# A fused attention and two-layer-block kernel: block 0's GpSimd low parts go to VectorE, all absolute values and q's readouts to ScalarE, and batch 1's attention is placed earlier

## The chip, the cores and the metric

The kernel runs on one core of a Trainium2 chip. The metric is device time in microseconds (us) of that core. The program has five engines that matter here: TensorE (PE; its weight loads are PEld), VectorE (DVE), ScalarE (ACT), GpSimd (POOL) and SyncE (SP), which issues the DMAs.

## The reference

All inputs arrive as 64-bit floats, which the kernel reads as pairs of 32-bit words. What is computed, cut to its core:

```python
p_packed = sm_attn(p, k, v)              # 32 packed queries for each head; softmax over 576 tokens
out = sm_attn(q, p_packed, p_packed)     # 576 queries over 32 packed keys; 8 batches, 8 heads of 64
x = out.transpose(0, 2, 1, 3)            # 4608 tokens x 512
h = x @ w_in                             # 512 -> 2048
g = np.where(h > 0, h, exp(min(h, 0)) - 1)
x2 = g @ w_out                           # 2048 -> 512
y = ((x2 @ w_a) * (x2 @ w_b)) @ w_out2   # 512 -> 1536 -> 512
```

## The kernel before, in words

The first part works by batch: eight blocks of 32 steps. A step takes one half h of a batch's tokens (288) and one slice f of 128 of the 2048 hidden columns. It makes `h` = w_in' a (`l1`, line 458, six matmuls: high x high, high x low, low x high over two row groups), the activation (`act1`: ge on ScalarE, lines 466 and 467, gf on VectorE, line 470, its high part gr on ScalarE, line 472, its low part, line 474) and, two steps later, the second layer (`l2`, line 480: twelve matmuls into four accumulators x2a). Every fp32 product is three products of high and low parts. In block 0 the slices come in two halves, so that the first steps need only a part of the weights: steps 0 to 15 take f 0 to 7 of both token halves, steps 16 to 31 take f 8 to 15. A tile `h0_0_8` is that of batch 0, half 0, f 8, and so of step 16.

The products of w_in with the packed values (`wp`, line 245, four for each batch, wp0_0 to wp0_3 for batch 0) take the place of w_in in the first layer: each is read out by ScalarE (line 82) and VectorE (line 83) into a ring `wr` of five pairs. So l1 of four steps waits for one wp. The attention of batch b + 1 runs within block b: score products (s1), exponentials e, their transposes (aT), packed values (pp, line 306, and its readout pps, line 320), their transposes (ppT), the second scores (s2), a softmax over 32 keys (lines 343 to 370), and the four wp. The tiles pT, s1, aT, pp, ppT, s2 and wp share one pair of PSUM banks (`pair_of_banks`, one buffer).

Block 0 also converts the weights of the first part from 64-bit words: `convert`, 16 tiles of w_in (`win`) and 16 of w_out (`wm_o`), 128 x 512 each. Step u0 takes the absolute value of the high word, two of three on ScalarE (line 134), the third on VectorE (line 136), and scales the low word on ScalarE; u1 clamps (line 140) and shifts (line 141); u2 puts the sign in (line 144) and adds the low word on GpSimd (line 147); u3, for w_out alone, splits into a high part (ScalarE, line 151) and a low part (line 152). The low parts of w_out, and those of gr in every second step of block 0, are computed by GpSimd. The transposed q is read out of PSUM in `qkT_tokens` (line 214), alternately by ScalarE and VectorE.

The order of the work: each piece has a time in half steps (`put`), two for each step, with block b's step s at 64b + 2s; `run_until` emits what is due as the steps go by, and a piece whose chain is stuck waits. `issue_until` emits what a step needs if it has not come yet. Batch 1's attention stands at 24 + 0.9t for its own times t from 0 to 64, and its last items (t > 64) at t + 2.3. In block 0 the order on each engine is then the framework scheduler's; from block 1 on TensorE, VectorE and ScalarE keep the order of the code.

After the eight blocks comes the second part (lines 808 to 860), which no edit touches.

Of the kernel before, what the change touches and what calls it, by code (L numbers as in the profile page):

```python
# [16 lines left out]
U32 = mybir.dt.uint32  # L17
# [3 lines left out]
P = 128  # L21
# [4 lines left out]
def program(tc, q, k, v, p, w_in, w_out, w_a, w_b, w_out2, out):  # L26
# [8 lines left out]
    nc = tc.nc  # L35
# [25 lines left out]
    with ctx:  # L61
# [4 lines left out]
        stage = ctx.enter_context(tc.tile_pool(name="stage", bufs=NSTAGE))  # L66
# [4 lines left out]
        at = at_stack.enter_context(tc.tile_pool(name="at", bufs=1, reuse_waits="tile"))  # L71
# [15 lines left out]
        wout_r = [w1.tile([P, 2, DM], F32R, name=f"wout{f}") for f in range(NF)]  # L87
# [4 lines left out]
        win = at.tile([P, NJ, FF], F32, name="win")  # L92
# [27 lines left out]
                )  # L120
            return t

        def convert(t, key, mags, dst=None, parts=None, pool_lo=True, on_act=True, store=None):

            w = t.bitcast(U32).rearrange("p (n t) -> p n t", t=2)
            low, high = w[:, :, 0], w[:, :, 1]
            pool, n = mags
            m = pool.tile([P, 512], U32, tag="wmag", name=f"wm_{key}", bufs=n) if dst is None else dst  # L130

            def u0():
                if on_act:
                    nc.scalar.activation(m.bitcast(F32), high.bitcast(F32), AF.Abs)
                else:
                    nc.vector.tensor_scalar(m, high, 0x7FFFFFFF, None, ALU.bitwise_and)
                nc.scalar.activation(low.bitcast(I32), low, AF.Copy, scale=2.0 ** -29)

            def u1():
                nc.vector.tensor_scalar(m.bitcast(F32), m.bitcast(F32), F64_MIN, F64_MAX, ALU.max, ALU.min)  # L140
                nc.vector.tensor_scalar(m, m, 3, 0x3FFFFFF8, ALU.logical_shift_left, ALU.bitwise_and)

            def u2():
                nc.vector.scalar_tensor_tensor(  # L144
                    m, high, 0xC0000000, m, op0=ALU.bitwise_and, op1=ALU.bitwise_or
                )
                nc.gpsimd.tensor_tensor(m.bitcast(I32), m.bitcast(I32), low.bitcast(I32), op=ALU.add)

            def u3():
                f = m.bitcast(F32)  # L150
                nc.scalar.copy(parts[:, 0, :], f)
                (nc.gpsimd if pool_lo else nc.vector).tensor_tensor(
                    parts[:, 1, :], f, parts[:, 0, :].bitcast(F32), op=ALU.subtract
                )

            def u4():
                nc.sync.dma_start(store, m.bitcast(F32))

            return [u0, u1, u2] + ([] if parts is None else [u3]) + ([] if store is None else [u4])
# [35 lines left out]
        def qkT_tokens(b, which, jj):  # L195

            if jj == 0:
                st[b, which + "T"] = at.tile([P, NJ, S], F32, tag="qkT", name=f"{which}T{b}")
            dst = st[b, which + "T"]
            t, tail = st[b, which, jj]  # L200
            for i in range(2):
                o = bank("h", 2, f"{which}Tp{b}_{jj}{i}")
                for c in range(4):
                    for r in range(2):
                        nc.tensor.matmul(
                            o[r * D:(r + 1) * D, c * P:(c + 1) * P],
                            t[:, 2 * i + r, c, :],
                            ident,
                            start=True,
                            stop=True,  # L210
                            tile_position=(0, r * D),
                        )
                copy = nc.vector.tensor_copy if i else nc.scalar.copy
                copy(
                    dst[:, 2 * jj + i, :4 * P].rearrange("p (n c) -> p c n", c=4),
                    o.rearrange("p (c n) -> p c n", c=4),
                )
            o = bank("h", 2, f"{which}Tt{b}_{jj}")
            n = S - 4 * P
            for i in range(2):  # L220
                nc.tensor.transpose(o[:, i * n:(i + 1) * n], tail[:, i * P:(i + 1) * P], ident[:n, :n])
            nc.vector.tensor_copy(
                dst[:, 2 * jj:2 * jj + 2, 4 * P:], o[:, :2 * n].rearrange("p (i n) -> p i n", i=2)
            )
# [236 lines left out]
                    n += 1  # L461
            return t

        def act1(t, key, run, pool_lo=False):
            e = m1.tile([P, HS], F32, tag="ge", name=f"ge{key}")
            nc.scalar.activation(e, t[:, :HS], AF.Relu, scale=-1.0)  # L466
            nc.scalar.activation(e, e, AF.Exp, scale=-1.0)  # L467
            run(0)
            g = m1.tile([P, HS], F32, tag="gf", name=f"gf{key}")
            nc.vector.scalar_tensor_tensor(g, e, -1.0, t[:, :HS], op0=ALU.add, op1=ALU.max)  # L470
            gr = m1.tile([P, 2, HS], F32R, tag="gr", name=f"gr{key}", bufs=4)
            nc.scalar.copy(gr[:, 0, :], g)  # L472
            run(1)
            (nc.gpsimd if pool_lo else nc.vector).tensor_tensor(gr[:, 1, :], g, gr[:, 0, :].bitcast(F32), op=ALU.subtract)  # L474
            return gr

        def l2(acc, f, gr, first, last):
# [65 lines left out]
                clock[0] += 1  # L543
                run_until(clock[0])

        def conveyor(convs, mags, late, on_act):


            convs = sorted(convs, key=lambda x: x[0])
            words = {}  # L550

            def load(i):
                if i < len(convs):
                    words[i] = load_words(convs[i][1], convs[i][2])

            def step(i, n):
                _, _, key, dst, parts, pool_lo = convs[i]
                if n == 0:
                    words[i] = convert(words[i], key, mags[i % len(mags)], dst, parts, pool_lo, bool(on_act) and i % on_act != 0)
                if n < len(words[i]):  # L560
                    words[i][n]()
                    if n + 1 == len(words[i]):
                        done.add(key)
                if n == 2:
                    load(i + NSTAGE)

# [39 lines left out]
        for n, (kind, x, j) in enumerate(order):  # L606
            if n < 4:
                t = -44 + 4 * n
            elif n < 16:
                t = -34 + 1.5 * (n - 4)  # L610
            else:
                t = 12 + 2.5 * (n - 16)
            if kind == "i":
                convs.append((t, w_in[j * P:(j + 1) * P, x * 512:(x + 1) * 512], f"i{x}_{j}",
                              win[:, j, x * 512:(x + 1) * 512].bitcast(U32), None, True))
            else:
                convs.append((t, w_out[x * P:(x + 1) * P, :], f"o{x}", None, wout_r[x], True))
        conveyor(convs, [(stage, 2), (at, 1), (stage, 2)], 4, 3)
        for b in range(1, B):
            for t, fn, takes, frees in attention(b):  # L620
                late = t > 64
                if b == 1:
                    t = 24 + 0.9 * max(t, 0) if not late else t + 2.3
                put(2 * NF * 2 * (b - 1) + t, fn, chain=(b, late), takes=takes, frees=frees)


        def m1_block(b):
            half = NF // 2 if b == 0 else NF
            order = [(h, f) for f0 in range(0, NF, half) for h in range(2) for f in range(f0, f0 + half)]
            for s, (h, f) in enumerate(order):  # L630
                first, last = f % half == 0, f % half == half - 1
                if first:
                    acc = []
                t0 = 4 * NF * b + 2 * s
                t = l1(b, h, f)
                gr = act1(t, f"{b}_{h}_{f}", lambda n: run_until(t0 + n), b == 0 and s % 2 == 0)
                pend.append((b, h, f, gr, acc, first, last, f // half + 1 if half < NF else 0))
                if len(pend) > 2:
                    run_pend()
# [293 lines left out]
```

## Time and profile before

| | |
|---|---|
| median of three runs | 1662.57 us (1661.4, 1662.57, 1662.66) |
| the profiled execution | 1660.11 us, span 1658.1 us |
| PE busy | 1576.9 us (95%), PEld 1442.4 us (87%) |
| DVE busy | 1034.2 us (62%) |
| ACT busy | 710.3 us (43%) |
| POOL busy | 206.3 us (12%) |

The first five of the profile's 40 slices of 41.5 us have TensorE busy by tenths 5, 4, 8, 8, 9, VectorE 6, 9, 9, 8, 5 and GpSimd 2, 5, 5, 5, 0; almost all others have TensorE at 9. The block borders used below are the starts of the first h of step 16 (134.70 us), of block 1 (183.79 us) and of block 2 (287.73 us). Busy shares are averages over stages with different limits, so the stretches are to be read one by one.

### The profile page before, as it was taken

How to read it: one execution, taken by the hardware profiler on the slowest of the kernel's cores; microseconds unless marked ns; L12 is line 12 of the kernel's file. 1: busy time of each engine (PE TensorE's matmuls, PEld its weight loads, DVE VectorE, ACT ScalarE, POOL GpSimd, SP SyncE). 2: the span in 40 equal slices, each digit the busy share in tenths (PEclk: the TensorE clock that was granted, in tenths of full speed). 3: DMA queues.
4: the chain of work that ended last, by engine and by line, in shares of the span. 5: the costliest groups of instructions: out<-in, count | busy, mean ns of one | idle time of the engine just before them, and what ended most of it. 6: DMA issues, size and time to landing. Idle time of an engine off the chain costs nothing.

```text
span 1658.1 us, 27473 instructions
## 1 busy us (share of the span) xinstructions
PE 1576.9 (95%) x10824; PEld 1442.4 (87%) x10824; DVE 1034.2 (62%) x2035; ACT 710.3 (43%) x1566; POOL 206.3 (12%) x154
## 2 busy tenths in 40 slices
PE   5488989999999999999989999999999999999999
PEld 4277788989999898989878899989989999998997
DVE  6998567776767676755699834535445553463452
ACT  4566456666666666666533312212222221231211
POOL 2555000001000000002175200000000000000000
PEclk8599999999999999999999999999999999999999
DMA  7655322626252534114175735545545563553541
GB/s 235 176 156 147 107 61 74 158 68 146 82 139 83 134 93 120 50 47 167 48 271 229 276 126 214 187 156 191 209 159 184 192 226 139 185 198 114 212 181 39
DMA packets 214785, 247.95 MB, mean 150 GB/s; under 512 B 150144, under 2 KB 180864, under 8 KB 205440
## 3 DMA queue, kind: packets, MB, share of 16 engines
q1 hardware_dynamic: 214656, 246.19, 46.2%
q8 instruction: 85, 1.39, 0.3%
q14 instruction: 44, 0.36, 0.1%
HBM read 194.64 MB, written 51.51 MB: 148 GB/s over the span
## 4 chain that ended last, share of the span: by engine, by line
PE 79%; DVE 7%; issue 4%; ACT 3%; POOL 2%; DMA 2%; SPq 1%; DVEq 0%; POOLq 0%; ACTq 0%
PE x2a L480 21%; PE o L852 17%; PE B L808 12%; PE h L458 10%; PE C L808 8%; PE A L808 8%; POOL e L714 2%; DVE gf L470 1%; DVE wr L83 1%; SPq L169 1%; POOL wo L797 1%; ACT wr L82 1%; PE pp L306 1%; DVE win L144 1%; DVE gr L474 1%
## 5 line engine op out<-in xcount | busy, mean ns | idle before, releaser
L480 PE MATMUL x2a<-gr,wout 128*128 128x288 f32 x3072 | 466.9, 301 | 4.4 <-DVE gr L474 2.8
L480 PEld LDWEIGHTS x2a<-gr,wout 128*128 128x128 f32 x3072 | 425.0, 190 | 47.0 <-issue 16.2
L852 PE MATMUL o<-wo,c 128*128 128x512 f32 x1296 | 307.7, 391 | 0.0
L852 PEld LDWEIGHTS o<-wo,c 128*128 128x128 f32 x1296 | 242.5, 188 | 47.9
L808 PE MATMUL B<-s,e 128*128 128x384 f32 x1296 | 262.4, 337 | 8.2 <-DVE u L833 4.3
L458 PE MATMUL h<-a,wr 128*128 128x288 f32 x1536 | 251.8, 300 | 11.8 <-DVE gf L470 6.0
L458 PEld LDWEIGHTS h<-a,wr 128*128 128x128 f32 x1536 | 222.2, 192 | 19.3 <-DVE gf L470 10.6
L808 PEld LDWEIGHTS B<-s,e 128*128 128x128 f32 x1296 | 227.6, 188 | 12.6 <-DVE u L833 7.2
L808 PE MATMUL A<-s,e 128*128 128x384 f32 x864 | 175.4, 337 | 1.8 <-ACT p L831 1.8
L808 PE MATMUL C<-s,e 128*128 128x384 f32 x864 | 173.3, 334 | 0.0
L470 DVE SCALAR_TENSOR_TENSOR gf<-ge,h 128x288 f32<-128x288 f32 x256 | 113.6, 444 | 93.3 <-ACT ge L467 90.6
L472 ACT CAST gr<-gf 128x288 fp32r<-128x288 f32 x256 | 110.4, 432 | 140.7 <-DVE gf L470 139.3
L808 PEld LDWEIGHTS A<-s,e 128*128 128x128 f32 x864 | 154.3, 188 | 7.9 <-ACT p L831 2.1
L808 PEld LDWEIGHTS C<-s,e 128*128 128x128 f32 x864 | 152.2, 188 | 0.3 <-ACT p L835 0.3
L474 DVE TENSOR_TENSOR gr<-gf,gr 128x288 fp32r<-128x288 f32 x240 | 124.1, 517 | 34.5 <-ACT gr L472 31.7
L466 ACT ACTIVATE ge<-h 128x288 f32<-128x288 f32 x256 | 104.2, 408 | 78.6 <-PE h L458 77.7
L82 ACT CAST c<-u 128x384 fp32r<-128x384 f32 x72 | 36.9, 512 | 230.1 <-DVE u L841 230.1
L838 DVE TENSOR_TENSOR v<-p,B 128x384 f32<-128x384 f32 x72 | 39.8, 552 | 142.6 <-PE B L808 142.6
L467 ACT ACTIVATE ge<-ge 128x288 f32<-128x288 f32 x256 | 113.8, 445 | 7.5
L833 DVE TENSOR_TENSOR u<-p,B 128x384 f32<-128x384 f32 x72 | 39.7, 551 | 104.2 <-PE B L808 104.1
L831 ACT COPY p<-A 128x384 f32<-128x384 f32 x72 | 34.5, 479 | 117.9 <-PE A L808 117.9
L835 ACT COPY p<-C 128x384 f32<-128x384 f32 x72 | 34.5, 479 | 103.5 <-PE C L808 103.5
(346 smaller groups left out, 1501.7 us busy)
## 6 DMA issues: line engine op xcount, KB each, us to landing
e<-ed SPq DMA_DIRECT2D x60, 1792.0 KB, 7.2
ed<-e SPq DMA_DIRECT2D x12, 1792.0 KB, 6.4
x2d<-x2s SPq DMA_DIRECT2D x32, 288.0 KB, 2.4
out_dram<-osb SPq DMA_DIRECT2D x36, 256.0 KB, 2.0
v<-in_v_dram SPq DMA_DIRECT2D x8, 1024.0 KB, 8.3
wst_i<-in_moe_w_in_dram SPq DMA_DIRECT2D x16, 512.0 KB, 4.6
wst_o<-in_moe_w_out_dram SPq DMA_DIRECT2D x16, 512.0 KB, 4.6
kst<-in_k_dram SPq DMA_DIRECT2D x112, 72.0 KB, 2.5
```

What stands on the lines that cost most here:

```text
L82: nc.scalar.copy(hi, src)
L458: nc.tensor.matmul(t[:, :HS], w[:, wi, o * P:(o + 1) * P], x[:, xi, :], start=(n == 0), stop=(n == 5))
L466: nc.scalar.activation(e, t[:, :HS], AF.Relu, scale=-1.0)
L467: nc.scalar.activation(e, e, AF.Exp, scale=-1.0)
L470: nc.vector.scalar_tensor_tensor(g, e, -1.0, t[:, :HS], op0=ALU.add, op1=ALU.max)
L472: nc.scalar.copy(gr[:, 0, :], g)
L474: (nc.gpsimd if pool_lo else nc.vector).tensor_tensor(gr[:, 1, :], g, gr[:, 0, :].bitcast(F32), op=ALU.subtract)
L480: nc.tensor.matmul(acc[d][:, :HS], wout_r[f][:, wi, d * P:(d + 1) * P], gr[:, xi, :], start=(first and n == 0), stop=(last and n == 2),)
L808: nc.tensor.matmul(bank[:, :HT], es[f][:, E_OF[i], wi, k * P:(k + 1) * P], ss[i][:, xi, k, :], start=(first and n == 0), stop=(n == 5), sk ...
L833: nc.vector.tensor_tensor(u, p1, pB, op=ALU.add)
L838: nc.vector.tensor_tensor(v, p1, pB, op=ALU.add)
L852: nc.tensor.matmul(acc, cr[:, xi, t * P:(t + 1) * P], wo[f][:, wi, :], start=(f == 0 and n == 0), stop=(f == NF2 - 1 and n == 2),)
```

## The change

The low parts of w_out and of gr in block 0 are computed by VectorE, as those of all other blocks are. All absolute values go to ScalarE. VectorE keeps the readouts of k alone; q's two of that kind go to ScalarE. Batch 1's attention stands at 14 + 0.78t; its items with t between 32 and 36 stand at 48 + t - 33, or 49 if that is later. The times of its last items are unchanged.

```diff
@@ convert
             def u0():
-                if on_act:
-                    nc.scalar.activation(m.bitcast(F32), high.bitcast(F32), AF.Abs)
-                else:
-                    nc.vector.tensor_scalar(m, high, 0x7FFFFFFF, None, ALU.bitwise_and)
+                nc.scalar.activation(m.bitcast(F32), high.bitcast(F32), AF.Abs)
                 nc.scalar.activation(low.bitcast(I32), low, AF.Copy, scale=2.0 ** -29)
...
             def u3():
                 f = m.bitcast(F32)
                 nc.scalar.copy(parts[:, 0, :], f)
-                (nc.gpsimd if pool_lo else nc.vector).tensor_tensor(
-                    parts[:, 1, :], f, parts[:, 0, :].bitcast(F32), op=ALU.subtract
-                )
+                nc.vector.tensor_tensor(parts[:, 1, :], f, parts[:, 0, :].bitcast(F32), op=ALU.subtract)
...
@@ qkT_tokens
-                copy = nc.vector.tensor_copy if i else nc.scalar.copy
+                copy = nc.vector.tensor_copy if i and which == "k" else nc.scalar.copy
...
@@ act1
-            (nc.gpsimd if pool_lo else nc.vector).tensor_tensor(gr[:, 1, :], g, gr[:, 0, :].bitcast(F32), op=ALU.subtract)
+            nc.vector.tensor_tensor(gr[:, 1, :], g, gr[:, 0, :].bitcast(F32), op=ALU.subtract)
...
@@ the placing of batch 1
                 late = t > 64
                 if b == 1:
-                    t = 24 + 0.9 * max(t, 0) if not late else t + 2.3
+                    t = t + 2.3 if late else max(48 + t - 33, 49) if 32 < t < 36 else 14 + 0.78 * max(t, 0)
                 put(2 * NF * 2 * (b - 1) + t, fn, chain=(b, late), takes=takes, frees=frees)
...
@@ m1_block
-                gr = act1(t, f"{b}_{h}_{f}", lambda n: run_until(t0 + n), b == 0 and s % 2 == 0)
+                gr = act1(t, f"{b}_{h}_{f}", lambda n: run_until(t0 + n))
```

The edit takes lines out: lines 140, 141, 144, 147 and 152 of before are 137, 138, 141, 144 and 149 of after, and from there on a line stands five higher (480 is 475).

VectorE before, where the first words of w_out are converted (wm_o0 to wm_o2 are the words, nm the reciprocals that scale pps):

```order
L136 TENSOR_SCALAR wm_o1_528<-wst_o1_488 128x512
L140 TENSOR_SCALAR wm_o0_513<-wm_o0_513 128x512
L140 TENSOR_SCALAR wm_o1_528<-wm_o1_528 128x512
L141 TENSOR_SCALAR wm_o0_513<-wm_o0_513 128x512
L141 TENSOR_SCALAR wm_o1_528<-wm_o1_528 128x512
L140 TENSOR_SCALAR wm_o2_556<-wm_o2_556 128x512
L144 SCALAR_TENSOR_TENSOR wm_o0_513<-wst_o0_472,wm_o0_513 128x512
L144 SCALAR_TENSOR_TENSOR wm_o1_528<-wst_o1_488,wm_o1_528 128x512
L320 TENSOR_SCALAR pps0_407<-pp0_362,nm0_0_277 128x64
L320 TENSOR_SCALAR pps0_407<-pp0_362,nm0_1_281 128x64
L141 TENSOR_SCALAR wm_o2_556<-wm_o2_556 128x512
L144 SCALAR_TENSOR_TENSOR wm_o2_556<-wst_o2_496,wm_o2_556 128x512
```

The same place after:

```order
L137 TENSOR_SCALAR wm_o0_513<-wm_o0_513 128x512
L138 TENSOR_SCALAR wm_o0_513<-wm_o0_513 128x512
L141 SCALAR_TENSOR_TENSOR wm_o0_513<-wst_o0_472,wm_o0_513 128x512
L137 TENSOR_SCALAR wm_o1_528<-wm_o1_528 128x512
L138 TENSOR_SCALAR wm_o1_528<-wm_o1_528 128x512
L137 TENSOR_SCALAR wm_o2_556<-wm_o2_556 128x512
L141 SCALAR_TENSOR_TENSOR wm_o1_528<-wst_o1_488,wm_o1_528 128x512
L138 TENSOR_SCALAR wm_o2_556<-wm_o2_556 128x512
L315 TENSOR_SCALAR pps0_407<-pp0_362,nm0_0_277 128x64
L315 TENSOR_SCALAR pps0_407<-pp0_362,nm0_1_281 128x64
L141 SCALAR_TENSOR_TENSOR wm_o2_556<-wst_o2_496,wm_o2_556 128x512
L149 TENSOR_TENSOR wout0_83<-wm_o0_513,wout0_83 128x512
L149 TENSOR_TENSOR wout1_84<-wm_o1_528,wout1_84 128x512
```

The absolute value of wm_o1 is gone from VectorE, and the low parts wout0 and wout1 stand there as subtractions.

TensorE before, in the first steps of block 1 (s1 is a score product of batch 2, wp1_1 batch 1's second weight product):

```order
L458 MATMUL h1_0_3_2133<-a2_1_0_0_1763,wr4_0_107 128x288 x3
L458 MATMUL h1_0_3_2133<-a2_1_0_1_1856,wr4_1_108 128x288 x3
L245 MATMUL s1_2_1__2146<-kT2_1660,pT2_2007 32x288 x8
L245 MATMUL wp1_1__2161<-win_163,ppT1_1577 32x512 x8
L480 MATMUL x2a1_0_0_0_2117<-gr1_0_1_2077,wout1_84 128x288 x3
L480 MATMUL x2a1_0_0_1_2118<-gr1_0_1_2077,wout1_84 128x288 x3
L480 MATMUL x2a1_0_0_2_2119<-gr1_0_1_2077,wout1_84 128x288 x3
L480 MATMUL x2a1_0_0_3_2120<-gr1_0_1_2077,wout1_84 128x288 x3
L458 MATMUL h1_0_4_2183<-a2_1_0_0_1763,wr0_0_99 128x288 x3
```

The same place after:

```order
L453 MATMUL h1_0_3_2184<-a2_1_0_0_1720,wr4_0_107 128x288 x3
L453 MATMUL h1_0_3_2184<-a2_1_0_1_1753,wr4_1_108 128x288 x3
L240 MATMUL s1_2_1__2197<-kT2_1707,pT2_2080 32x288 x8
L475 MATMUL x2a1_0_0_0_2168<-gr1_0_1_2113,wout1_84 128x288 x3
L475 MATMUL x2a1_0_0_1_2169<-gr1_0_1_2113,wout1_84 128x288 x3
L475 MATMUL x2a1_0_0_2_2170<-gr1_0_1_2113,wout1_84 128x288 x3
L475 MATMUL x2a1_0_0_3_2171<-gr1_0_1_2113,wout1_84 128x288 x3
L453 MATMUL h1_0_4_2225<-a2_1_0_0_1720,wr0_0_99 128x288 x3
```

wp1_1 no longer stands there, nor do wp1_2 and wp1_3, which stood behind h1_0_5 and h1_0_7; all three stand in block 0 now.

TensorE before, at batch 0's third weight product (x2a0_0 is the second layer of steps 0 to 7):

```order
L480 MATMUL x2a0_0_0_3_698<-gr0_0_5_807,wout5_88 128x288
L245 MATMUL wp0_2__1217<-win_163,ppT0_439 32x512 x8
L480 MATMUL x2a0_0_0_3_698<-gr0_0_5_807,wout5_88 128x288
L458 MATMUL h0_1_0_886<-a2_0_1_0_893,wr0_0_99 128x288 x3
L458 MATMUL h0_1_0_886<-a2_0_1_1_898,wr0_1_100 128x288 x3
```

The same product after, with the start of step 16 (h0_0_8):

```order
L475 MATMUL x2a0_1_0_3_1054<-gr0_1_6_1213,wout6_89 128x288
L240 MATMUL wp0_2__1317<-win_163,ppT0_439 32x512 x8
L475 MATMUL x2a0_1_0_0_1051<-gr0_1_6_1213,wout6_89 128x288 x2
...
L475 MATMUL x2a0_1_0_3_1054<-gr0_1_7_1290,wout7_90 128x288 x2
L453 MATMUL h0_0_8_1342<-a2_0_0_0_520,wr2_0_103 128x288 x2
```

It stood ahead of step 8's h and stands now between the second layers of steps 14 and 15, just ahead of step 16, which uses it.

## Rows read from the trace of the kernel before

**Rows 1.** Busy time by stretch (first line: the columns); x counts instructions.
```profile
core 0: us, PE busy (x) PEld busy (x) DVE busy (x) ACT busy (x) POOL busy (x), PEclk, DMA share, GB/s
62.40:134.70 72.30, 53.45 (x420) 44.51 (x420) 70.84 (x121) 44.18 (x101) 38.10 (x30) 0.78 0.56 151
134.70:183.80 49.10, 46.93 (x372) 41.36 (x371) 34.75 (x83) 27.22 (x66) 18.99 (x17) 0.99 0.52 130
183.80:287.70 103.90, 96.39 (x843) 84.31 (x844) 66.61 (x152) 60.88 (x142) 7.93 (x6) 0.97 0.30 81
287.70:376.30 88.60, 88.36 (x799) 80.87 (x798) 64.00 (x149) 58.55 (x141) 7.88 (x6) 1.00 0.43 109
```

**Rows 2.** VectorE's groups, 0 to 190 us: busy us, mean ns | idle before.
```profile
L144 DVE SCALAR_TENSOR_TENSOR win<-wst_i,win 128x512 uint32<-128x512 uint32 x16 | 14.1, 889 | 0.1
L140 DVE TENSOR_SCALAR wm_o<-wm_o 128x512 f32<-128x512 f32 x16 | 13.8, 864 | 1.0 <-ACT wm_o L134 0.9
L144 DVE SCALAR_TENSOR_TENSOR wm_o<-wst_o,wm_o 128x512 uint32<-128x512 uint32 x16 | 13.4, 843 | 0.2
L141 DVE TENSOR_SCALAR wm_o<-wm_o 128x512 uint32<-128x512 uint32 x16 | 11.7, 734 | 0.2
L141 DVE TENSOR_SCALAR win<-win 128x512 uint32<-128x512 uint32 x16 | 11.4, 720 | 0.1
L140 DVE TENSOR_SCALAR win<-win 128x512 f32<-128x512 f32 x16 | 10.3, 652 | 0.0
...
L136 DVE TENSOR_SCALAR wm_o<-wst_o 128x512 uint32<-128x512 uint32 x6 | 4.4, 734 | 0.0
L136 DVE TENSOR_SCALAR win<-wst_i 128x512 uint32<-128x512 uint32 x5 | 4.2, 845 | 3.2 <-DMA wst_i<-in_moe_w_in_dram 3.2
...
L214 DVE COPY qT<-qTp 128x512 f32<-128x512 f32 x2 | 2.1, 1068 | 0.0
```

**Rows 3.** GpSimd's groups, 0 to 190 us, columns as in Rows 2.
```profile
L152 POOL TENSOR_TENSOR wout<-wm_o,wout 128x512 fp32r<-128x512 f32 x16 | 24.0, 1509 | 0.7 <-ACT wout L151 0.7
L147 POOL TENSOR_TENSOR win<-win,wst_i 128x512 int32<-128x512 int32 x16 | 22.7, 1428 | 40.1 <-DVE win L144 38.2 <-DMA qsn<-in_q_dram 1.1 <-DVE nm L276 0.7
L147 POOL TENSOR_TENSOR wm_o<-wm_o,wst_o 128x512 int32<-128x512 int32 x16 | 22.0, 1376 | 17.2 <-DVE wm_o L144 9.8 <-DMA kst<-in_k_dram 4.1 <-ACT aT L295 1.1
L474 POOL TENSOR_TENSOR gr<-gf,gr 128x288 fp32r<-128x288 f32 x16 | 13.7, 855 | 38.9 <-ACT gr L472 29.8 <-PE x2a L480 9.1
```

**Rows 4.** Durations by line: ns shortest/middle/longest, first and last start.
```profile
L140 DVE TENSOR_SCALAR win<-win x16: 358/414/1523, 17.5 to 98.8; 128x512 f32<-128x512 f32 x16
...
L144 DVE SCALAR_TENSOR_TENSOR wm_o<-wst_o,wm_o x16: 674/680/1671, 43.0 to 149.0; 128x512 uint32<-128x512 uint32 x16
...
L474 DVE TENSOR_TENSOR gr<-gf,gr x240: 405/452/1608, 80.3 to 814.0; 128x288 fp32r<-128x288 f32 x120
```

**Rows 5.** Timeline of GpSimd and VectorE, 125.5 to 131 us: start, us.
```profile
126.01 2.87 POOL L152 TENSOR_TENSOR wout<-wm_o,wout 128x512 fp32r<-128x512 f32 x2
126.37 1.38 DVE L140 TENSOR_SCALAR wm_o<-wm_o 128x512 f32<-128x512 f32 x1
129.09 0.68 DVE L83 TENSOR_TENSOR wr<-wp__1417,wr 128x512 fp32r<-128x512 f32 x1
```

**Rows 6.** TensorE's timeline at five places; idle before and its end in brackets.
```profile
129.87 1.08 PE L306 MATMUL pp<-v,aT 128*32 128x64 f32 x32 [4.08 <-issue]
...
134.70 1.31 PE L458 MATMUL h<-a,wr 128*128 128x288 f32 x6
...
183.79 0.53 PE L458 MATMUL h<-a,wr 128*128 128x288 f32 x2 [0.71 <-ACT wr L82]
...
198.42 1.09 PE L245 MATMUL wp__2161<-win,ppT 64*32 64x512 f32 x16 [1.25 <-ACT e L262]
...
287.73 0.95 PE L458 MATMUL h<-a,wr 128*128 128x288 f32 x6
```

**Rows 7.** ScalarE's absolute values of w_in, 0 to 190 us, columns as in Rows 2.
```profile
L134 ACT ACTIVATE win<-wst_i 128x512 f32<-128x512 f32 x11 | 7.5, 681 | 5.6 <-DMA wst_i<-in_moe_w_in_dram 5.6
```

**Rows 8.** The second layer's matmuls over the whole run, columns as in Rows 2.
```profile
L480 PE MATMUL x2a<-gr,wout 128*128 128x288 f32 x3072 | 466.9, 301 | 4.4 <-DVE gr L474 2.8
```

More of the change, by code (lines that the diff above doesn't have):

```diff
@@ L121, in load_words, with convert @@
             return t
-        def convert(t, key, mags, dst=None, parts=None, pool_lo=True, on_act=True, store=None):
+        def convert(t, key, mags, dst=None, parts=None, store=None):
             w = t.bitcast(U32).rearrange("p (n t) -> p n t", t=2)
@@ L462, in l1, with act1 @@
             return t
-        def act1(t, key, run, pool_lo=False):
+        def act1(t, key, run):
             e = m1.tile([P, HS], F32, tag="ge", name=f"ge{key}")
@@ L544, in issue_until, with conveyor @@
                 run_until(clock[0])
-        def conveyor(convs, mags, late, on_act):
+        def conveyor(convs, mags, late):
             convs = sorted(convs, key=lambda x: x[0])
@@ L556, in step @@
             def step(i, n):
-                _, _, key, dst, parts, pool_lo = convs[i]
+                _, _, key, dst, parts = convs[i]
                 if n == 0:
-                    words[i] = convert(words[i], key, mags[i % len(mags)], dst, parts, pool_lo, bool(on_act) and i % on_act != 0)
+                    words[i] = convert(words[i], key, mags[i % len(mags)], dst, parts)
                 if n < len(words[i]):
@@ L614, in program @@
                 convs.append((t, w_in[j * P:(j + 1) * P, x * 512:(x + 1) * 512], f"i{x}_{j}",
-                              win[:, j, x * 512:(x + 1) * 512].bitcast(U32), None, True))
+                              win[:, j, x * 512:(x + 1) * 512].bitcast(U32), None))
             else:
-                convs.append((t, w_out[x * P:(x + 1) * P, :], f"o{x}", None, wout_r[x], True))
-        conveyor(convs, [(stage, 2), (at, 1), (stage, 2)], 4, 3)
+                convs.append((t, w_out[x * P:(x + 1) * P, :], f"o{x}", None, wout_r[x]))
+        conveyor(convs, [(stage, 2), (at, 1), (stage, 2)], 4)
         for b in range(1, B):
```

## The prediction

> **What bounds the kernel now.** I read the table of engine busy time first, then the 40 slices, and then busy time by stretch. Over the whole run TensorE is busy 95% of the span, so only places where it is not can give time back. The slices put them at the start: TensorE has 5, 4 and 8 tenths in the first three slices and 9 nearly everywhere else. By stretch [rows 1]: from 62.4 us to the first h of step 16 [rows 6] TensorE is busy 53.45 of 72.30 us, at a granted clock of 0.78, while VectorE is busy 70.84 of those 72.30. VectorE bounds that stretch. From step 16 to block 1 TensorE is busy 46.93 of 49.10 us at 0.99: TensorE bounds it. Block 1 lasts 103.90 us, and block 2, with the same 32 steps and all of its work in place, 88.60 us at clock 1.00. So block 1 carries 15.3 us more than a steady block. Before block 1, and in it, lie all the edits; from block 2 on no instruction is changed or moved, and the rest of the run I carry over as it is.
>
> Next, why VectorE is full. The groups of its conversion work [rows 2] have means from 0.65 to 0.89 us, but the same instructions' shortest and middle durations are 0.36 and 0.41 us (clamp, line 140) and 0.67 and 0.68 us (sign, line 144) [rows 4]. They are either clean or long. The timeline shows what a long one is [rows 5]: a 1.38 us clamp starts at 126.37, inside a pair of GpSimd low parts that began at 126.01, and the low part that VectorE computes after them at 129.09 takes 0.68 us. TensorE's pp at 129.87 had stood 4.08 us [rows 6]: it needs the PSUM pair that this VectorE instruction frees. GpSimd has four such groups in block 0 [rows 3]: the adds (line 147), 22.7 and 22.0 us, and the low parts, 24.0 (line 152) and 13.7 us (line 474).
>
> **The change part by part.** I count instructions in the two orders and price them by rows.
>
> *Up to step 16's gf, on VectorE.* It gains 14 w_out low parts and 9 gr low parts, and loses 10 absolute values and the two q readouts. A w_out low part has no row on VectorE; the nearest is line 83's subtraction of the same shape, 0.68 us [rows 5]. A gr low part is 0.452 us by the middle of VectorE's own 240 [rows 4]. An absolute value I take at the clean 0.414 us of line 140, though its groups say 0.73 and 0.85 us [rows 2]: that part of its time is a stall, and a stall may pass to the next instruction. A q readout is 1.07 us [rows 2]. That is 14 x 0.68 + 9 x 0.452 - 10 x 0.414 - 2 x 1.07 = +7.3 us. Two more pps, two more x2s and two fewer wr come to nothing (+0.1).
>
> *The stalls.* The six clamp, shift and sign groups take 74.7 us together [rows 2]; clean they would take 32 x (0.414 + 0.414 + 0.68) = 48.3, with the shift taken as long as the clamp. The excess is 26.4 us, and 8.6 - 11 x 0.414 = 4.1 more in the absolute values: 30.5. I divide it by GpSimd's time: low parts are 37.7 of 82.4 us [rows 3], 46%, so 13.9 us; those that leave before step 16 are 14 x 1.509 + 9 x 0.855 = 28.8 of the 37.7 us, so 10.6 us. Bounds: nothing, if the adds stall as much as both did (then +7.3), and all of the 30.5 x 76% = 23.2 us (then -15.9). I take 7.3 + 0.1 - 10.6, **-3 us**, nearest to the share. VectorE is full there, so this is path.
>
> The Trainium skill (SBUF — State Buffer, section "Who interferes with whom") says that VectorE and GpSimd share a pair of ports as an exclusive lock, and that a two-input VectorE instruction with both inputs in SBUF contends with a GpSimd instruction that reads SBUF. The long instructions of [rows 5] agree with that; but by it the new low parts, which have two SBUF inputs, become victims of the adds that remain. The page Perfetto Trace Analysis (section "Optimizing Scalar/DVE Operations") advises offloading a saturated VectorE; this edit loads it. By both rules the stretch gets longer, which is the first rival below.
>
> *ScalarE.* It gains 11 absolute values at 0.681 us [rows 7] and two readouts of about VectorE's 1.07 us: 9.6 us. It is busy 44.18 of 72.30 us in the crowded stretch [rows 1]; this lies beside VectorE's work. It would cost at most what is added to chains that TensorE awaits, two readouts: 0 to +2.1, taken as 0.
>
> *The order around step 16.* wp0_2 now stands just ahead of step 16's h, behind 32 second-layer products that stood after it: 32 x 0.301 = 9.6 us [rows 8]. They leave the second half and fill TensorE's 18.9 idle us in the first, so the border moves and the sum does not. What can appear is a refill: step 16's second layer is not ready when TensorE comes to it. Bounds 0 and one steady step, 88.60 / 32 = 2.8 us; two more h and a score product stand between, so I take 0.
>
> *Second half of block 0.* Four more wp stand there, 4 x 1.09 [rows 6], and pp loses 24 of the trace's products, 24 x 1.08 / 32 [rows 6]: 4.4 - 0.8 = **+3.5 us** of TensorE work in a stretch that TensorE bounds. VectorE gets 7 gr and 2 w_out low parts and 8 wr low parts: 34.75 + 3.2 + 1.4 + 5.4 = 44.7 of 52.6 us, so I add no wait. Bounds: 0, if the waits of 2.2 us (49.10 - 46.93) take them in, and +11.5, if the waits of batch 1's attention come along (rival 3).
>
> *Block 1.* Three wp are gone, 3.3 us, with what waited for them: wp1_1 stood 1.25 us for ScalarE's e [rows 6]. The attention of batch 1 is over when block 1 begins, and the order of its first steps is that of block 2. I take the whole difference, **-15.3 us**; bounds -15.3 and the wp alone with a slower clock, about -8 (96.39 - 88.36 of busy time).
>
> *SP.* The k loads of batch 2 now stand ahead of the last w_out words in its queue; those words are wanted late in block 0, and DMA is at 0.52 there [rows 1]: 0.
>
> Sum: -3 + 3.5 - 15.3 = -14.8. The profiled execution took 1660.11 us, so 1645.3; the median of the three runs, 1662.57, lies 2.5 above it, so **1647.5 us**.
>
> **Rivals.**
> 1. *The stalls stay.* The adds (44.7 us of GpSimd) go on catching VectorE, and the low parts are caught too. For it: the adds are 54% of GpSimd's time here, and a two-input subtraction of VectorE has been as long as 1.608 us [rows 4]. Against it: GpSimd's load falls by 46%. Then the first stretch is +7.3, the sum -4.4, the median 1658.
> 2. *More goes than the low parts' share.* The absolute values' 4.1 us of stall vanish with them, since ScalarE's take 0.681 us [rows 7] against 0.845 on VectorE, and the second half's 2.2 us of waits close: -21.1, 1641.
> 3. *Batch 1's waits move into block 0.* Of block 1's 15.3 us, 12.0 are waits and clock; if 8 reappear in the second half of block 0, where a batch's softmax chains now stand closer together (0.78 of a half step instead of 0.9): -6.8, 1656. For it: the single PSUM pair makes pp and wp wait already [rows 6].
> 4. *Slower: VectorE becomes the bound of the second half too.* It has 85% of that stretch by the count above, against 72% in block 2 (64.00 of 88.60). The first stretch did 53.45 x 0.78 = 41.7 us of full-speed TensorE work in 72.30, a rate of 58%. The second half holds 46.93 + 3.5, about 50 us: at 58% it lasts 86 us, at 66% 76 us, +27 in place of +3.5, which makes the total +8 and the median 1671. It decides from 67.4 us on (a rate of 74%). Against it: 85% is not 98%, and no conversion with its adds is left after 149 us [rows 4].
>
> That the change doesn't do what it says I exclude: the orders show all three wp gone from block 1.
>
> **How the numbers follow.** Forecast 0.45, rivals 0.14, 0.18, 0.15 and 0.08. The forecast with its small bounds is 1642 to 1653; the range goes from below rival 2 to just past rival 1: **1637 to 1659**. A difference under 0.2% (3.3 us) cannot be told from none here. Faster: the forecast, rivals 2 and 3, and somewhat over a third of rival 1, whose 1658 lies near that bound: 0.84. No change: the rest of rival 1: 0.07. Slower: rival 4 and a little for what I do not see: 0.09.
>
> **What would show it.** GpSimd left with 32 adds and no low part in block 0; the means of lines 140 and 141 (137 and 138 after) falling from 0.65 to 0.86 to about 0.55; VectorE no longer 98% busy before step 16 and the clock there above 0.78; the first h of block 1 again near 183.8 us; block 1 lasting 88.6 to 90 us. The forecast is wrong if the new low parts take well over 0.7 us, if block 1 starts after 190 us, or if block 1 keeps more than 95 us.

## The result and the profile after

The changed kernel takes 1647.32 us (median of four runs, 1643.5 to 1649.01) against 1662.62 us: the ratio is 0.9906, with an interval of 0.9887 to 0.9924. Measured again later, it took 1647.09 us, ratio 0.9914 (0.9901 to 0.9928). Forecast was 1647.5.

Busy time by stretch after, cut at the first h of block 0, of step 16, of block 1, of block 2 and of block 3 (columns as in [rows 1]):

```profile
core 0: us, PE busy (x) PEld busy (x) DVE busy (x) ACT busy (x) POOL busy (x), PEclk, DMA share, GB/s
56.20:129.70 73.50, 55.92 (x459) 47.14 (x460) 67.75 (x136) 47.21 (x107) 24.16 (x17) 0.84 0.58 153
129.70:182.00 52.30, 46.48 (x379) 38.37 (x378) 40.96 (x95) 30.77 (x74) 2.94 (x2) 0.97 0.41 111
182.00:270.60 88.60, 87.95 (x798) 80.72 (x797) 62.29 (x147) 57.25 (x136) 7.89 (x6) 1.00 0.35 96
270.60:359.30 88.70, 88.42 (x799) 80.92 (x798) 64.11 (x149) 58.61 (x141) 7.88 (x6) 1.00 0.43 109
```

Block 1 lasts 88.60 us, exactly a steady block, where it lasted 103.90 [rows 1]. In this pair of traces the gain lies there: block 1 begins at 182.03 us, 1.8 us earlier than before [rows 6], so block 0 gained hardly anything. The experiments show that this is where the gain ends up, and not all of what makes it.

What was in those 15 us is read from what TensorE waited for in block 1, before (engine, operation and line, then what it waited for: us in all, times, longest):

```profile
PE wp__2318 L245 <- DVE nm L276: 2.3, 1, 2.3
PE aTp L286 <- DVE wr L83: 1.5, 1, 1.5
PE wp__2161 L245 <- ACT e L262: 1.2, 1, 1.2
PE aT5p L294 <- ACT aT L288: 1.2, 1, 1.2
PE h L458 <- ACT wr L82: 0.9, 2, 0.7
PE h L458 <- DVE wr L83: 0.6, 3, 0.2
PE x2a L480 <- ACT ge L466: 0.5, 1, 0.5
```

and after:

```profile
PE aT5p L289 <- ACT aT L283: 0.6, 1, 0.6
```

The waits fall from 8.2 to 0.6 us, and TensorE's idle time in block 1 from 7.5 to 0.6 us (length less busy time in the rows). Its busy time falls by 8.4 us. Three wp at 1.09 us are 3.3 of these. The clock, 0.97 there before and 1.00 after, makes an estimated 3: 3% of 103.9 us. The last 2 have no source in these rows. The waits belonged to the wp and to batch 2's attention, which queued with them for the one PSUM pair.

VectorE's conversions up to 190 us (columns as in [rows 2]) and GpSimd's:

```profile
L149 DVE TENSOR_TENSOR wout<-wm_o,wout 128x512 fp32r<-128x512 f32 x16 | 12.6, 795 | 1.3 <-ACT wout L148 1.3
L141 DVE SCALAR_TENSOR_TENSOR win<-wst_i,win 128x512 uint32<-128x512 uint32 x16 | 12.1, 753 | 0.2
L137 DVE TENSOR_SCALAR wm_o<-wm_o 128x512 f32<-128x512 f32 x16 | 11.7, 733 | 1.3 <-ACT wm_o L133 1.2
L141 DVE SCALAR_TENSOR_TENSOR wm_o<-wst_o,wm_o 128x512 uint32<-128x512 uint32 x16 | 11.6, 727 | 0.1
L138 DVE TENSOR_SCALAR win<-win 128x512 uint32<-128x512 uint32 x16 | 11.5, 721 | 0.2
L137 DVE TENSOR_SCALAR win<-win 128x512 f32<-128x512 f32 x16 | 9.3, 583 | 2.0 <-ACT win L133 2.0
L138 DVE TENSOR_SCALAR wm_o<-wm_o 128x512 uint32<-128x512 uint32 x16 | 8.6, 536 | 0.2
```

```profile
L144 POOL TENSOR_TENSOR win<-win,wst_i 128x512 int32<-128x512 int32 x16 | 22.5, 1408 | 42.9 <-DVE win L141 34.4 <-ACT e L257 3.2 <-DVE mx L353 3.1
L144 POOL TENSOR_TENSOR wm_o<-wm_o,wst_o 128x512 int32<-128x512 int32 x16 | 22.4, 1397 | 55.7 <-DVE wm_o L141 34.4 <-ACT wr L82 8.4 <-ACT gr L467 4.3
```

The low parts are gone from GpSimd [rows 3], and the six clamp, shift and sign groups on VectorE (lines 137, 138 and 141) fell from 74.7 to 64.8 us [rows 2], not to their clean 48. The adds still stall VectorE, and on TensorE's path. The timeline after, from 116 us (start, us):

```profile
116.34 1.52 POOL L144 TENSOR_TENSOR wm_o<-wm_o,wst_o 128x512 int32<-128x512 int32 x1 [1.71 <-ACT gr L467]
116.63 1.52 DVE L137 TENSOR_SCALAR wm_o<-wm_o 128x512 f32<-128x512 f32 x1
118.07 0.45 DVE L469 TENSOR_TENSOR gr<-gf,gr 128x288 fp32r<-128x288 f32 x1
...
118.57 1.32 PE L475 MATMUL x2a<-gr,wout 128*128 128x288 f32 x8 [1.39 <-DVE gr L469]
```

A clamp caught by an add takes 1.52 us in place of 0.42; the gr low part behind it on VectorE is late, and TensorE waits 1.39 us for it.

To compare the experiments I cut every trace at the same four TensorE marks. The tail is what follows the first h of block 2. The last column is worked out from the durations of VectorE's instructions up to step 16's gf. The stall is the time beyond the lower quartile of their kind (line and shape), over all that overlap a GpSimd instruction; clean is what is left of the durations' sum. The rest is the time up to that gf less this sum. It is not VectorE's idle time: neighbouring instructions overlap in the trace, by 11 to 15 us in all (17 with the adds on VectorE), and the idle time is longer than the rest by that much: 16.9 us before and 21.9 after. The medians were not all measured beside each other, so the ratios given below are safer than differences of medians.

| kernel | median us | step 16's h | block 1 starts | block 1 lasts | tail | VectorE to step 16's gf: clean + stall + rest |
|---|---|---|---|---|---|---|
| before | 1662.62 | 134.7 | 183.8 | 103.9 | 1370.3 | 96.7 + 36.7 + 3.6 |
| before, second profile | 1662.89 | 135.5 | 184.7 | 103.9 | 1373.2 | 96.9 + 36.5 + 4.5 |
| changed | 1647.32 | 129.7 | 182.0 | 88.6 | 1374.2 | 104.5 + 20.8 + 8.4 |
| changed, second profile | 1647.09 | 131.6 | 184.0 | 88.6 | 1373.5 | 104.4 + 20.2 + 11.0 |
| placement alone | 1649.38 | 135.1 | 185.1 | 88.6 | 1373.5 | 97.6 + 35.2 + 5.6 |
| moves alone | 1652.21 | 125.8 | 174.0 | 104.5 | 1373.4 | 103.7 + 23.9 + 3.7 |
| w_out low on GpSimd | 1650.81 | 132.7 | 186.1 | 88.7 | 1374.2 | 95.1 + 31.6 + 10.3 |
| gr low on GpSimd | 1645.17 | 130.8 | 182.0 | 88.7 | 1373.2 | 101.0 + 24.8 + 8.9 |
| both low on GpSimd | 1650.59 | 134.7 | 186.2 | 88.6 | 1373.6 | 91.4 + 34.8 + 11.4 |
| absolute values on VectorE | 1653.33 | 135.1 | 188.9 | 88.6 | 1373.2 | 108.4 + 26.3 + 6.3 |
| adds on VectorE | 1652.78 | 129.5 | 183.4 | 89.3 | 1379.1 | 125.2 + 0.0 + 10.8 |
| 14 + 0.85t | 1649.64 | 128.1 | 180.5 | 94.0 | 1373.3 | 104.5 + 20.6 + 8.6 |
| wp0_2 early | 1639.98 | 124.8 | 180.4 | 88.5 | 1374.1 | 101.0 + 21.2 + 9.1 |
| wp0_2 early, gr low on GpSimd | 1640.27 | 123.8 | 176.7 | 88.6 | 1371.9 | 98.2 + 25.0 + 5.8 |

### The profile page after: what moved, and what is told of

The parts are those of the page before. It is cut to its first block, busy times and chain, and to the rows that moved or that the text cites. A ratio compares the mean times of both kernels' runs of the same rounds, so it can differ in the third digit from the quotient of the medians.

```text
span 1644.8 us, 27465 instructions
## 1 busy us (share of the span) xinstructions
PE 1569.8 (95%) x10824; PEld 1438.4 (87%) x10824; DVE 1025.1 (62%) x2054; ACT 717.0 (44%) x1579; POOL 168.8 (10%) x122
## 3 DMA queue, kind: packets, MB, share of 16 engines
q8 instruction: 85, 1.39, 0.3%
## 4 chain that ended last, share of the span: by engine, by line
PE 79%; DVE 6%; issue 4%; ACT 3%; DMA 3%; POOL 3%; SPq 2%; DVEq 0%; POOLq 0%; ACTq 0%
PE x2a L475 21%; PE o L846 17%; PE B L802 12%; PE h L453 10%; PE C L802 8%; PE A L802 8%; POOL e L708 2%; SPq L164 1%; POOL wo L791 1%; DMA wst_i<-in_moe_w_in_dram 1%; DVE gr L469 1%; DVE gf L465 1%; PE pp L301 1%; ACT gr L467 0%; DVE wr L83 0%
## 5 line engine op out<-in xcount | busy, mean ns | idle before, releaser
L475 PE MATMUL x2a<-gr,wout 128*128 128x288 f32 x3072 | 466.2, 300 | 10.3 <-DVE gr L469 6.4
L453 PE MATMUL h<-a,wr 128*128 128x288 f32 x1536 | 251.2, 299 | 16.9 <-DVE gf L465 8.6
L469 DVE TENSOR_TENSOR gr<-gf,gr 128x288 fp32r<-128x288 f32 x256 | 131.5, 514 | 34.4 <-ACT gr L467 32.3
L461 ACT ACTIVATE ge<-h 128x288 f32<-128x288 f32 x256 | 104.5, 409 | 74.0 <-PE h L453 73.3
```

The source lines that it names most:

```text
L453: nc.tensor.matmul(t[:, :HS], w[:, wi, o * P:(o + 1) * P], x[:, xi, :], start=(n == 0), stop=(n == 5))
L469: nc.vector.tensor_tensor(gr[:, 1, :], g, gr[:, 0, :].bitcast(F32), op=ALU.subtract)
L475: nc.tensor.matmul(acc[d][:, :HS], wout_r[f][:, wi, d * P:(d + 1) * P], gr[:, xi, :], start=(first and n == 0), stop=(last and n == 2),)
```

## The experiments

**The two halves apart.** The first keeps everything of before but the placing; the second keeps everything of the change but the placing.

```diff
-                    t = 24 + 0.9 * max(t, 0) if not late else t + 2.3
+                    t = t + 2.3 if late else max(48 + t - 33, 49) if 32 < t < 36 else 14 + 0.78 * max(t, 0)
```

> The kernel before with batch 1's attention at 14 + 0.78t alone; GpSimd, VectorE and ScalarE keep their shares of the conversions. Theory (two independent gains): block 1 falls from 103.9 to about 90 us as in the changed kernel, step 16's gf stays at 137 us give or take 2, and the total is 11 to 15 us below before, about 1649. Rival (the earlier attention needs the room that the moves make on VectorE): step 16's gf or the start of block 1 comes 5 to 8 us later than before, and the total is only 5 to 8 us below, about 1656.

Measured 1649.38 us, ratio 0.9930 (0.9918 to 0.9942). Block 1 lasts 88.6 us and step 16's gf comes at 138.4: the theory held.

> The changed kernel with batch 1's attention back at 24 + 0.9t: the moves between the engines alone. Theory: the stalls behind low parts (about 14 us of VectorE by overlap in the trace of before) go and the low parts' own time comes, so step 16's gf is 3 to 4 us earlier, block 1 keeps its 104 us, and the total is 3 to 4 us below before, about 1659. Rival (the placement hides a larger gain of the moves): step 16's gf 8 to 11 us earlier, total 1652 to 1654. Other rival (VectorE gains nothing, all comes from the placement): within 1 us of before.

Measured 1652.21 us, 0.9946 (0.9930 to 0.9962). The first rival held by its total, not by its step: step 16's gf comes 5.8 us earlier (131.3 against 137.0), not 8 to 11. Block 1 starts at 174.0 us, 9.8 earlier than before, and lasts 104.5. So the halves do not add: 12.2 and 9.4 us each against the 1661.61 us of before measured beside them, and 13.8 to 15.3 together. In block 0 the moves are worth 9.8 us at the old placement, and 1.2 to 3.1 at the new one (185.1 against 184.0 and 182.0). The second half of block 0, with the moves alone (columns as in [rows 1]):

```profile
125.80:174.00 48.20, 45.79 (x363) 39.97 (x361) 39.52 (x97) 27.53 (x67) 5.40 (x4) 1.00 0.57 142
```

**The parts of the moves put back one by one.** First the low parts of w_out, then of gr:

```diff
-                nc.vector.tensor_tensor(parts[:, 1, :], f, parts[:, 0, :].bitcast(F32), op=ALU.subtract)
+                nc.gpsimd.tensor_tensor(parts[:, 1, :], f, parts[:, 0, :].bitcast(F32), op=ALU.subtract)
```

> The changed kernel with the 16 low parts of w_out back on GpSimd. Theory (stalls behind GpSimd go by its time): about 9 us of VectorE stall come back and 12.6 us of VectorE's own work go, so step 16's gf moves by less than 3 us and the total stays within 3 us of the changed kernel's 1647. Rival (the w_out low parts carry the gain of the moves): 4 to 8 us slower, 1651 to 1655.

1650.81 us, 0.9935 (0.9923 to 0.9947), between the two: 3.5 us over the changed kernel, which is at the edge of the noise, since the two intervals meet (0.9923 to 0.9947 against 0.9887 to 0.9924 and 0.9901 to 0.9928). Step 16's gf comes 3.2 later: VectorE's clean time fell by 9.4, its stalls rose by 10.8 and the rest by 1.9.

```diff
-            nc.vector.tensor_tensor(gr[:, 1, :], g, gr[:, 0, :].bitcast(F32), op=ALU.subtract)
+            (nc.gpsimd if pool_lo else nc.vector).tensor_tensor(gr[:, 1, :], g, gr[:, 0, :].bitcast(F32), op=ALU.subtract)
...
+                gr = act1(t, f"{b}_{h}_{f}", lambda n: run_until(t0 + n), b == 0 and s % 2 == 0)
```

> The changed kernel with every second low part of gr in block 0 on GpSimd again. Theory (a GpSimd low part is 0.81 us and catches VectorE, and the second layer waits for it): about 5 us of stalls on VectorE come back and 16 x 0.45 go, and gr arrives 0.4 us later in every second step; block 1 starts 0 to 3 us later, total 1647 to 1650. Rival (they carry the gain of the moves): 4 to 7 us later, 1651 to 1654.

1645.17 us, 0.9901 (0.9886 to 0.9916): no slower than the changed kernel, and below the range of either account. Clean time falls by 3.5 and stalls rise by 4.0, as the theory has it. This part of the change bought nothing that these runs can tell.

For the absolute values:

```diff
-                nc.scalar.activation(m.bitcast(F32), high.bitcast(F32), AF.Abs)
+                if on_act:
+                    nc.scalar.activation(m.bitcast(F32), high.bitcast(F32), AF.Abs)
+                else:
+                    nc.vector.tensor_scalar(m, high, 0x7FFFFFFF, None, ALU.bitwise_and)
...
-                    words[i] = convert(words[i], key, mags[i % len(mags)], dst, parts)
+                    words[i] = convert(words[i], key, mags[i % len(mags)], dst, parts, on_act=i % 3 != 0)
```

> The changed kernel with every third absolute value on VectorE again, as before. Theory (clean price of 11 x 0.41 us, stalls of the adds pass on to them without growing): step 16's gf 3 to 5 us later, block 1's start 2 to 4 us later, total 1649 to 1651. Rival (their stall is theirs, 0.73 to 0.85 us each): 6 to 9 us later at step 16, total 1652 to 1655. Third (hidden beside TensorE): within 1 us.

1653.33 us, 0.9947 (0.9934 to 0.9959); step 16's gf 7.3 us later: clean time 3.9 more, stalls 5.5 more, the rest 2.1 less. The rival held by its times. But it blamed long absolute values, and they are not that long here (means of 0.60 and 0.64 us, with 2.2 us of stall in all):

```profile
L136 DVE TENSOR_SCALAR wm_o<-wst_o 128x512 uint32<-128x512 uint32 x6 | 3.6, 601 | 0.0
L136 DVE TENSOR_SCALAR win<-wst_i 128x512 uint32<-128x512 uint32 x5 | 3.2, 639 | 2.8 <-DMA wst_i<-in_moe_w_in_dram 2.8
```

The other 3.3 us of stalls stand on other instructions. The next run asks whether this price holds when GpSimd has the low parts (the edits of w_out's and of gr's low parts at once):

> The changed kernel with the low parts of both w_out and gr back on GpSimd: against the run with the placement alone (1649.4), only the absolute values and q's two readouts have moved. Theory (the absolute values' price, 7 us at step 16 by the run that put them back, is theirs wherever the low parts are): step 16's gf 5 to 8 us before that run's 138.4, total 1642 to 1645, which beats the changed kernel. Rival (the price depends on the low parts: while GpSimd holds them, a saved VectorE instruction only makes the next one stall): step 16's gf at 135 to 138.5, total 1647 to 1651, as in the run with w_out's low parts on GpSimd (1650.8).

1650.59 us, 0.9940 (0.9928 to 0.9952); step 16's gf at 137.7. My theory fell, and the rival held by its times, but not by its cause. Against the placement alone VectorE has 6.2 us less clean work up to step 16's gf, which is what ten absolute values and two readouts weigh by the prediction's prices (6.3). The stalls are the same (34.8 against 35.2): the saved work did not make others stall. VectorE stands idle instead, 23.0 us in place of 19.2, and step 16's gf comes 0.7 us sooner. What it then waits for is left open.

No run puts q's two readouts back alone. The first h of block 0 starts at 62.9 to 63.6 us in the three profiles that have them on VectorE, at 63.1 with the adds there, and at 56.2 to 58.6 in the ten others, whichever other part was put back. So a good part of this lead may be the readouts'; that is not shown. With the earlier placement it is gone by block 1, which starts at 186.2 us in the last run and at 185.1 with the placement alone.

**The adds on VectorE too.** On VectorE the trace shows this add as one custom operation on 16-bit halves. Whether its sums are exact no run here shows.

```diff
-                nc.gpsimd.tensor_tensor(m.bitcast(I32), m.bitcast(I32), low.bitcast(I32), op=ALU.add)
+                nc.vector.tensor_tensor(m.bitcast(I32), m.bitcast(I32), low.bitcast(I32), op=ALU.add)
```

> The changed kernel with the 32 adds of the low words also on VectorE (GpSimd then does nothing in the first block; VectorE's add is not exact for such integers, so the weights are off in their last bits). Theory (the remaining 23.8 us of stalls on VectorE come from the adds): no clamp, shift or sign instruction over 0.75 us; 32 adds of 0.5 to 0.9 us cost 16 to 29 us, so step 16's gf moves by -5 to +4 us and the total stays within 4 us of 1647. Rival (the long instructions have another cause, such as DMA writes or their operands): clamps of 1.4 us remain, and the total rises by 16 to 25 us.

1652.78 us, 0.9947 (0.9936 to 0.9959). The clamp's durations (ns: shortest/middle/longest, first and last start) and the add's groups:

```profile
L137 DVE TENSOR_SCALAR win<-win x16: 409/426/429, 16.0 to 90.7; 128x512 f32<-128x512 f32 x16
L137 DVE TENSOR_SCALAR wm_o<-wm_o x16: 407/420/427, 34.6 to 139.3; 128x512 f32<-128x512 f32 x16
```

```profile
L149 DVE TENSOR_TENSOR wout<-wm_o,wout 128x512 fp32r<-128x512 f32 x16 | 10.8, 673 | 0.0
L144 DVE CUSTOM_DVE_ANT_0 win<-wst_i,win 128x1024 uint16<-128x1024 uint16 x16 | 10.9, 682 | 0.0
L144 DVE CUSTOM_DVE_ANT_0 wm_o<-wst_o,wm_o 128x1024 uint16<-128x1024 uint16 x16 | 10.8, 681 | 0.0
```

Without GpSimd at work not one clamp exceeds 0.43 us, and w_out's low part takes 0.673 us in place of 0.795. That shows that the long instructions come from GpSimd. It buys nothing in block 0: clean time rises by 20.7 us and stalls fall by 20.8. With overlaps counted once VectorE is busy 108.0 us up to step 16's gf in place of 111.8, but idle for 6.1 us more, so this gf comes 2.3 us later. The total is worse by 5.5 us, outside my theory's 4. The adds of the later blocks are on VectorE too, and the tail is 5 us longer.

**The place of wp0_2.**

```diff
-                t = 64 + (-1, 7, 31, 39)[c] + (t - 54) % 3
+                t = 64 + (-1, 7, 23, 39)[c] + (t - 54) % 3
```

> The changed kernel with batch 0's third weight product (wp0_2) at half step 23 in place of 31, so that it stands before step 7's h and not just ahead of step 16. Theory (the refill at step 16 is part of what the earlier attention costs block 0): step 16's gf no longer lies 7.6 us behind step 15's, the three waits for gf after it (4.0 us of TensorE) shrink to under 1.5, and block 1 starts 2 to 4 us earlier; total 1643 to 1646. Rival (the waits only move to other steps, since VectorE's work before step 24 sets the pace): block 1 starts within 1 us of the changed kernel's, total 1646 to 1649.

1639.98 us, 0.9871 (0.9855 to 0.9887): 7 us faster than the changed kernel, more than expected: below the theory's 1643 to 1646. Step 16's gf comes right behind step 15's (131.0 and 131.3 us, where the changed kernel has 126.1 and 133.7). What TensorE waited for from step 16 to block 1, in the changed kernel:

```profile
PE h L453 <- DVE gf L465: 4.0, 3, 2.5
PE h L453 <- DVE wr L83: 0.4, 1, 0.4
PE s__1370 L240 <- ACT ppT L322: 0.4, 1, 0.4
```

and with wp0_2 early:

```profile
PE h L453 <- DVE gf L465: 3.5, 3, 1.8
PE wp__1797 L240 <- DVE t L338: 0.8, 1, 0.8
PE x2a L475 <- DVE gr L469: 0.5, 2, 0.3
```

The waits for gf did not shrink under 1.5 us as I expected, so the gain is not the refill as I pictured it. The profiled execution was this kernel's slowest of four (1644.83 us), with block 1 starting 1.6 us sooner than in the changed kernel's; what brings the other 5 us no trace of this kernel shows. Two things on record bear on it. Its mean granted clock was 0.978, where its three faster executions had 0.980 to 0.982 and the changed kernel's eight 0.976 to 0.980. And the last kernel below, with the same wp0_2, is as fast and was profiled in a fast execution (1638.97 us): there block 1 starts at 176.7 us, 5.3 sooner than in the changed kernel's first profile. So part of the gain may be the clock, and most of it may lie before block 1; neither is shown for this kernel.

**The slope.**

```diff
-                    t = t + 2.3 if late else max(48 + t - 33, 49) if 32 < t < 36 else 14 + 0.78 * max(t, 0)
+                    t = t + 2.3 if late else max(48 + t - 33, 49) if 32 < t < 36 else 14 + 0.85 * max(t, 0)
```

> The changed kernel with 14 + 0.85t in place of 14 + 0.78t: wp1_3 then stands in block 1, behind its first h; everything else of batch 1 stays in block 0. Theory (block 1's loss goes by the batch 1 work left in it): one product of 1.09 us and its wait of 0 to 2.3 us come back in block 1, which lasts 90 to 92 us, block 0 gets 1 to 3 us shorter, total within 2 us of 1647. Rival (any batch 1 work left in block 1 upsets the order of its first ten steps): block 1 lasts 95 us or more, total over 1650.

1649.64 us, 0.9932 (0.9920 to 0.9945). Block 1 lasts 94.0 us, between the two accounts and nearer the rival's 95: one wp left in it costs 5.4 us, of which its own time is 1.1. The listed waits are 2.6 us longer than in the changed kernel (3.2 against 0.6), and the clock there is 0.98 in place of 1.00, an estimated 1.9 us of the 94. What TensorE waited for there:

```profile
PE s__2147 L240 <- DVE wr L83: 1.2, 1, 1.2
PE x2a L475 <- DVE x2s L490: 1.0, 1, 1.0
PE aT5p L289 <- ACT aT L283: 0.6, 1, 0.6
PE wp__2070 L240 <- DVE pT L109: 0.4, 1, 0.4
```

**Second profiles, and both faster edits at once.**

> The kernel before once more, for a second profile. Theory (the 2 to 3 us by which every variant falls back between the end of the eighth block and the second part's 27th product o are this one profile's luck): the stretch from the last gf to o 27 lasts 2 to 3 us longer here than in the first profile, 58 to 59 us in place of 55.9. Rival (the change costs that there): 55.9 again, within 0.7.

The stretch took 58.7 us: luck of the first profile, by 2.9 us. An o product that began at 868.97 us in the first profile begins at 872.66 in this one, though block 2 began only 0.9 us later.

> The changed kernel once more, on the chip and in the call of the other three, for its spread and a second profile. Theory (the execution's own scatter lies in the second part and in the phase of stalls in the first): median 1645 to 1649; stalls on VectorE up to step 16's gf within 3 us of the first profile's 20.8; block 1 within 0.5 us of 88.7. Rival (the first profile was a lucky one): median 1650 or more.

1647.09 us; stalls 20.2, block 1 88.6. The theory held by its numbers. The 2.0 us by which block 1 starts later than in the first profile are not stalls: the rest is 11.0 us in place of 8.4.

> The changed kernel with wp0_2 at half step 23 and with every second low part of gr in block 0 on GpSimd again, the two edits that came out faster than the changed kernel or level with it. Theory (the two act on different stretches and add): 1637 to 1640. Rival (both spend the same slack of VectorE before step 16): within 2 us of the changed kernel's 1647, slower than wp0_2 alone (1640.0).

1640.27 us, 0.9877 (0.9862 to 0.9892): the gr edit adds nothing to wp0_2's, though nothing is lost either, so neither account holds as written. Both these kernels beat the two of the case: their intervals lie below that of the changed kernel's second measurement (0.9901 to 0.9928) and at the low end of the first's (0.9887 to 0.9924).

## Why the prediction was right

The place and size of the main term were right; in block 0 the sum came out by luck. Point by point, by its own steps. (The sum gives 1647.8 us; the 1647.5 on record is a slip of 0.3 that changes nothing.)

*Block 1, -15.3 us.* Measured 103.94 to 88.60 us by TensorE's marks. Block 1 lasts 88.5 to 88.7 us in all nine profiles with batch 1's four wp in block 0 and the adds on GpSimd, and 89.3 with the adds on VectorE. This term is shown: the placement alone brings it, and the moves alone do not.

*Step 16's gf, -3 us.* Measured -3.3 (137.0 to 133.7), but with other terms. The instructions added net 7.8 us of clean time (7.4 in the sum), the stalls fell by 15.9 (10.6), and the rest grew by 4.8 us, which the sum had at nothing. That the two errors cancel is luck.

*The stalls' share.* I divided the stall by GpSimd's time. Paired one by one up to 190 us in the traces, each with the GpSimd instruction that it overlaps most, 26.1 us of VectorE's excess lay beside adds and 13.8 beside low parts; after, 22.8 beside adds and none beside low parts. So the low parts' stall came out right (13.9 in the sum), but by two errors: the whole excess was 39.9 us, not 30.5, and the low parts' share 35%, not 46%. Up to step 16's gf 11.4 us beside low parts went (10.6 in the sum); against rival 1, they did not pass to the adds. Beside the adds 4.5 us went as well, and 4.1 us of stall had stood in the absolute values themselves, beside adds. On this rival 2 was right, though not with its total.

The Trainium skill's rule on the shared ports (SBUF — State Buffer, "Who interferes with whom") agrees with the run that has no GpSimd work. But about 15 of the 20.8 us of stall after stand on clamps and shifts, which have one input, and the two-input sentence that I quoted does not cover those. What I drew from it, that the new low parts become victims, came in small: 0.795 against 0.673 us. It did not decide. Its sentence that a reduce never contends agrees too: of VectorE's sixteen 128x288 reduces up to 190 us, six before and seven after ran beside a GpSimd instruction, and none took over 0.45 us.

*Offloading to a saturated VectorE.* In the prediction I read the Trainium skill's Perfetto Trace Analysis ("Optimizing Scalar/DVE Operations") as speaking against the low parts' move. It says more: offloading a saturated VectorE to ScalarE may make sense, and between GpSimd and VectorE it might not help. The runs agree with that: w_out's low parts are worth 3.5 us on VectorE, at the edge of the noise, and gr's nothing. What paid with them was the absolute values' move to ScalarE, 6 us, and only while the low parts are off GpSimd (the run with both low parts back shows no gain over the placement alone). Why it does not pay there stays open.

*Block 0 as a whole, +0.5 us.* Measured -1.8 in the first pair of profiles and -0.7 in the second. Two terms behind it were mis-sized and cancel. The moves by themselves bring 9.8 us at the start of block 1, where the sum had 3. The placement then takes 8.1 of it back (174.0 to 182.0 us; 10.0 by the second profile), where the sum had 3.5. Of the 8.1, 3.3 are the TensorE work of the three wp moved in. From block 0's first h to block 1 TensorE is busy 4.2 us longer than with the moves alone (55.92 + 46.48 against 52.44 + 45.79 us) and idle 4.1 us longer. Of this idle time 3.4 us lie behind step 16's h, where the clock is also 0.97 in place of 1.00. There TensorE waits 4.0 us for gf, where the refill was taken as 0 with a bound of 2.8; with the moves alone no such wait is listed. So rival 3 held in part: the placement costs block 0 4.6 to 6.5 us more than the sum had, of the 8 that this rival moved there. That wp0_2's place has a part in it is shown by the 7 us that its earlier time brings; which waits that removes is not.

*The rest, 0.* Between the first profiles the tail grew by 3.8 us. The second profile of before has 1373.2, so 2.9 of these are that execution's luck, and the rest is within the scatter of the runs, 1373.2 to 1374.2 in ten other profiles whose kernels differ only before block 2, and 1371.9 in one more.

*The signs named beforehand.* GpSimd kept its 32 adds and no low part; VectorE is busy 92% of the stretch before step 16 and no longer 98%; the clock there is 0.84; block 1 starts and lasts as said. The means of lines 137 and 138 did not all fall to about 0.55 us: they are 0.54 to 0.73. The new low parts took 0.795 us, above the 0.68 of the sum.

*Rival 4 did not come.* VectorE is busy 40.96 of 52.30 us in the second half, 78%, and that stretch was longer by 3.2 us while an estimated 9.6 us of second-layer products had left it; TensorE's busy share fell from 96% to 89%.

## What to carry to other kernels

Compare a stage that follows a start-up with the same stage in the steady state: the difference (here 15.3 us) is what a better placement of the start-up's left-overs can return in that stage, and it was returned to a tenth of a microsecond. Then ask what the earlier work costs where it goes: with the moves in place it cost block 0 8 to 10 us, so the placement itself was worth only 5 us beside them (1652.21 against 1647.3). Where two changes meet in one stretch, measure each alone: 9.4 and 12.2 us apart were 14 to 15 together. Before trusting a few microseconds in a single profile, take a second one of the kernel before.

## What was unexpected of the hardware

GpSimd's work here cost the busy VectorE about what VectorE needs to do it itself: up to step 16's gf the adds cost 20.8 us of stalls, and 20.7 us of clean time when moved (17.0 with overlaps counted once); gr's low parts 4.0 against 3.5 us; w_out's 10.8 against 9.4. And one leftover product of 1.09 us in block 1's first steps made that block 5.4 us longer, with the waits and the slower clock that came with it.
